# Attention in TensorE tiles of 64 rows by 32 columns, and blocks of 512 tokens, in front of two MLPs

## The chip, the core and the metric

The kernel runs on one core of one Trainium2 chip. The metric is the device time of one execution in microseconds. TensorE is called PE in the rows (PEld is its weight load), VectorE is DVE, ScalarE is ACT, GpSimd is POOL, and SyncE is SP, which issues the DMAs.

## The reference

For each of 4 batches and 8 heads, 768 queries of 64 elements are cut into 24 chunks of 32. A chunk attends to 8 memory keys and to its own neighbourhood: 16 keys to its left, its own 32, and 8 to its right, 64 keys in all (fewer at the ends). The result is a matrix of 3072 tokens by 512, which passes through two MLPs of hidden width 2048 in float32.

```
for c in range(nc):
    k_ctx = k[:, :, max(0, c*32 - 16) : min(S, c*32 + 32 + 8)]      # and v_ctx
    scores = scale * q_c @ concat(mem_k, k_ctx).T
    a = exp(scores - max(scores));  a = a / (sum(a) + 1e-9)
    out[:, :, c*32 : c*32 + 32] = a @ concat(mem_v, v_ctx)
x = out as [3072, 512]
x = silu(x @ w_in) @ w_out          # first MLP
x = relu(x @ w2_in)**2 @ w2_out     # second MLP
```

The weights are 64-bit floats; the kernel converts them on the chip.

## The kernel before, in words

**Precision.** The large products run as three matmuls in the format fp32r: each operand is split into a high part and a remainder (`high`, `low` pieces), and high x low, low x high, high x high are summed in PSUM. A matmul on plain float32 operands shows as two matmul records, each with a weight load of its own.

**First MLP and attention.** Tokens go in 8 blocks of 384 (`TB`). `mlp(j)` takes 16 steps a block; a step has 12 matmuls of 384 columns into the hidden tile (`hidden`, L738 to L740), Silu and the split (L746, L750, L753), and 12 matmuls back (`back`, L771 to L773). The attention of block j+1 is issued among the steps of block j. Its unit is one head of one block: 4 groups of 96 queries (3 chunks) against the 128 keys that any of the three sees. Blocks 0 and 1 take the plain path (`plain_pair`): float32 scores with the mask as three extra rows (L360), transposes on TensorE (L488), Exp (L494), the product with the values with a column of ones for the sums (L500), the division, and a transpose back (L527). The other six blocks take a path with fp32r scores (operands made at L328 to L342, matmuls L362 and L363), four Exp a unit (L389), the division (L396 to L398), eight 32x32-block transposes a unit on VectorE (L413), and one float32 product for two heads (L432), in which each head writes its own 64 output columns. Two heads are a pair; a block has four pairs.

**Block 0** runs while the weights of the first MLP arrive and are converted (`convert`, L545 to L610), so TensorE, ScalarE and VectorE are all loaded there. Before it stands a start-up stretch with nothing but the attention of block 0.

**Second MLP.** It runs in 6 blocks of 512 tokens: the first product by seven products of half size (`stage_in`, L904, 42 matmuls of 256 columns), the second by 12 matmuls of 512 columns a half (`stage_out`, L995 to L997). Its weights are converted during the last blocks of the first MLP (`convert_out`) and around the start of the second (`convert_forms`).

**The order of the work.** Every piece is an entry of a graph with a due time, its engine's cost, what it comes after, and the buffers that it takes from rings (`Graph.order`). A list scheduler places the ready piece with the earliest due time on a free engine; the placed order is the program order of each engine, so an engine waits in that order for what is late. A ring's next user comes after the users of the buffer that it takes over, and starts behind the ring's previous taker. PSUM has 8 banks: `acc` 4, `ph` 2, `sc` 1, `po` 1.

Of the kernel before, what the change touches and what calls it, by code (L numbers as in the profile page):

```python
# [13 lines left out]
F32 = mybir.dt.float32  # L14
# [12 lines left out]
GC = 3  # L27
GQ = GC * CHUNK
GK = NMEM + LEFT + GQ + RIGHT
NG = S // GQ  # L30
UG = 4
TB = UG * GQ
NHALF = NG // UG
NB = B * NHALF
NT = B * S
DM = H * D
# [4 lines left out]
NU = NB * H  # L41
QW, KW, VW = TB, UG * GK, UG * (D + 1)
MASKED = -float(2 ** 100)
# [8 lines left out]
F32_UNITS = 2 * H  # L52
# [8 lines left out]
PRODUCTS = (1, 6, 5, 7, 2, 3, 4)  # L61

# [120 lines left out]
def chunk_attention_two_mlps(ctx, tc, units, values, weights, consts, out):  # L183
# [12 lines left out]

    for i in range(FT):
        pool(f"w{i}")
    for tag, n in (
        ("raw", 3), ("v", 4), ("pr", 2), ("pts", 2), ("qk", 1), ("k20", 1), ("k21", 1),  # L200
        ("x", 2), ("g", 3), ("wraw", 2), ("wu", 4), ("wr", 3), ("y", 2), ("nm", 3), ("sm", 3),
    ):
        pool(tag, n)
    for tag, n in (("acc", 4), ("ph", 2), ("sc", 1), ("po", 1)):
        pool(tag, n, bass.MemoryType.PSUM)
# [17 lines left out]
    split = [G.buf(t) for t in ("qk", "k20", "k21")]  # L223
    qk = take(split[0], [P, 2 * QW + KW], F32R)
    q1, k1, q2 = qk[:, :QW], qk[:, QW:QW + KW], qk[:D + GC, QW + KW:]
    k2 = [take(b, [D + GC, KW], F32R) for b in split[1:]]


    FIRST, SLOW = 32.0, 95.0
    STEP1 = 4.97  # L230
# [11 lines left out]
    def unit_due(u):  # L242
        j, h = divmod(u, H)
        if j == 0:
            return FIRST - 2.2 * (H - 1 - h)
        at, to = step_due(j - 1, 0), step_due(j, 0)
        return at + (to - at) * (h + 1) / H - 2.0
# [3 lines left out]
    last_scores, pairs = [], []  # L251

    def const_loads():

        done = []
        for n, (dst, at) in enumerate([(q2, 0), (k2[0], QW), (k2[1], QW + KW)]):
            width, c = dst.shape[1], G.buf("v")

            def load(e, at=at, width=width, c=c):
                t = take(c, [P, KW], BF16)  # L260
                nc.sync.dma_start(out=t[D:D + GC, :width], in_=consts[:, at:at + width])

            def copy(e, dst=dst, width=width, c=c):
                nc.gpsimd.tensor_copy(dst[D:D + GC], c.tile[D:D + GC, :width])

            due = unit_due(F32_UNITS) - 40 + 3 * n
            a = G.add({"SP": 0.45}, due, load, new=[c], size=4000)
            done.append(G.add({"POOL": 1.3}, due + 2, copy, [a], uses=[c, *split]))
        return done

    turned = []

    def sees(c, k):

        first = NMEM + c * CHUNK
        last = NMEM + LEFT + (c + 1) * CHUNK + RIGHT
        return k * CHUNK < NMEM or k * CHUNK < last and (k + 1) * CHUNK > first

    def cleared(due):

        pts = G.buf("pts")

        def zero(e):
            t = take(pts, [P, TB], F32).rearrange("p (g q) -> p g q", g=UG)
            for k in range(GK // CHUNK):
                for c in range(GC):
                    if not sees(c, k):
                        ks, qs = slice(k * CHUNK, (k + 1) * CHUNK), slice(c * CHUNK, (c + 1) * CHUNK)
                        nc.gpsimd.memset(t[ks, :, qs], 0.0)

        return pts, G.add({"POOL": 1.2}, due, zero, new=[pts]), []

    def attend(u, masks, pair):
        j, h = divmod(u, H)
        half, plain, due = j % NHALF, u < F32_UNITS, unit_due(u)
        rows = D + GC if plain else P

        raw = G.buf(f"w{FT - H + h}" if j == 0 else "raw")
        v = raw if j == 0 else G.buf("v")

        def load(e):
            take(raw, [P, QW + KW + VW * (j == 0)], F32)
            r = D if plain else P
            nc.sync.dma_start(out=raw.tile[:r, :QW + KW], in_=units[u, :r])
            if plain:
                nc.sync.dma_start(out=raw.tile[D:rows, :QW + KW], in_=units[u, D:rows])

        def load_v(e):
            if j:
                take(v, [P, VW], F32)  # L310
            nc.sync.dma_start(out=v.tile[:, v_at:], in_=values[u])

        v_at = 0 if j else QW + KW
        got = G.add({"SP": 0.8 if plain else 0.4}, due - 28, load, new=[raw],
                    size=rows * (QW + KW) * 4)
        if j == 0:
            got_v = G.add({"SP": 0.4}, due - 22, load_v, uses=[raw], size=P * VW * 4)
            got_v.behind.append(got)
        else:
            got_v = G.add({"SP": 0.4}, due - 22, load_v, new=[v], size=P * VW * 4)  # L320
        ready = [got]
        if not plain:
            free = [got, *last_scores, *masks]

            def high(e):
                t = raw.tile
                q, k = t[:, 0:QW], t[:, QW:QW + KW]
                nc.gpsimd.tensor_scalar(q1, q, SCALE, 1.0, op0=ALU.mult, op1=ALU.mult)  # L328
                nc.gpsimd.tensor_scalar(k1, k, 1.0, 1.0, op0=ALU.mult, op1=ALU.mult)
                nc.gpsimd.tensor_scalar(  # L330
                    q2[0:D], q[0:D], SCALE, 1.0, op0=ALU.mult, op1=ALU.mult
                )

            def low_q(e):
                q = raw.tile[:, 0:QW]
                nc.vector.scalar_tensor_tensor(
                    q1[D:P], q[D:P], SCALE, f(q1[D:P]), op0=ALU.mult, op1=ALU.subtract
                )

            def low_k(e):  # L340
                k = raw.tile[:, QW:QW + KW]
                nc.vector.tensor_tensor(k2[half][0:D], k[0:D], f(k1[0:D]), op=ALU.subtract)  # L342

            a = G.add({"POOL": 1.9}, due - 17, high, free, uses=[raw, *split])
            b = G.add({"DVE": 0.75}, due - 15, low_q, [a], uses=[raw, *split], port=True)
            c = G.add({"DVE": 0.75}, due - 14.5, low_k, [a], uses=[raw, *split], port=True)
            ready = [b, c]

        tag = "acc" if j == 0 else "sc"
        sc, nm, pr = G.buf(tag), G.buf("nm"), G.buf("pr")  # L350
        sm = None if plain else G.buf("sm")

        def score(e):
            t = take(sc, [GQ, KW], F32)
            for g in range(UG):
                o = t[:, g * GK:(g + 1) * GK]
                qs, ks = slice(g * GQ, (g + 1) * GQ), slice(g * GK, (g + 1) * GK)
                if plain:
                    r = raw.tile[:rows, :QW + KW]
                    nc.tensor.matmul(o, r[:, qs], r[:, QW:][:, ks], start=True, stop=True)  # L360
                else:
                    nc.tensor.matmul(o, q2[:, qs], k2[half][:, ks], start=True, stop=False)  # L362
                    nc.tensor.matmul(o, q1[:, qs], k1[:, ks], start=False, stop=True)  # L363

        def top(e):
            t = take(nm, [GQ, UG], F32)
            nc.vector.tensor_reduce(
                t, sc.tile.rearrange("p (g k) -> p g k", g=UG), axis=AX.X, op=ALU.max, negate=True
            )

        s = G.add({"PE": 1.1 if plain else 0.7}, due - 11, score, ready, new=[sc],
                  uses=[raw] if plain else [raw, *split])
        last_scores[:] = [] if plain else [s]
        m = G.add({"DVE": 0.72}, due - 10, top, [s], new=[nm], uses=[sc])
        if plain:
            pair.append((u, sc, nm, pr, v, v_at, m, got_v))
            if h % 2:
                pairs.append((pair[:], due))
                pair.clear()

            while h % 2 and len(pairs) > (j == 0 and h < H - 1):
                plain_pair(*pairs.pop(0))
            return

        def exp(e):
            p = take(pr, [GQ, UG, GK], F32)
            s = take(sm, [GQ, UG], F32)
            for g in range(UG):
                nc.scalar.activation(  # L389
                    p[:, g, :], sc.tile[:, g * GK:(g + 1) * GK], AF.Exp,  # L390
                    bias=nm.tile[:, g:g + 1], accum_out=s[:, g:g + 1],
                )

        def norm(e):
            p, s = pr.tile, sm.tile
            nc.vector.tensor_scalar(s, s, EPS, 1.0, op0=ALU.add, op1=ALU.mult)  # L396
# [7 lines left out]
        if not turned:  # L404
            turned.extend(cleared(due - 40) for _ in range(2))
# [14 lines left out]
        if h % 2 == 0:  # L420
            return
# [714 lines left out]
```

## Time and profile before

| what | value |
|---|---|
| median of 3 runs (lowest to highest) | 1181.97 us (1181.8 to 1183.61) |
| profiled execution, its own time | 1181.42 us |
| its span, first to last instruction | 1179.4 us |
| busy: PE, DVE, ACT, POOL | 99%, 70%, 52%, 19% |
| DMA, share of 16 engines | 31.2% |

Busy time of TensorE counts a matmul from its issue to its modelled end, and matmuls overlap; so the pace is read from the distance between starts, not from the duration of one.

### The profile page before, as it was taken

How to read it: one execution, taken by the hardware profiler on the slowest of the kernel's cores; microseconds unless marked ns; L12 is line 12 of the kernel's file. 1: busy time of each engine (PE TensorE's matmuls, PEld its weight loads, DVE VectorE, ACT ScalarE, POOL GpSimd, SP SyncE). 2: the span in 40 equal slices, each digit the busy share in tenths (PEclk: the TensorE clock that was granted, in tenths of full speed). 3: DMA queues.
4: the chain of work that ended last, by engine and by line, in shares of the span. 5: the costliest groups of instructions: out<-in, count | busy, mean ns of one | idle time of the engine just before them, and what ended most of it. 6: DMA issues, size and time to landing. Idle time of an engine off the chain costs nothing.

```text
span 1179.4 us, 19661 instructions
## 1 busy us (share of the span) xinstructions
PE 1162.7 (99%) x7360; PEld 1098.5 (93%) x7360; DVE 831.2 (70%) x1748; ACT 616.7 (52%) x1296; POOL 221.6 (19%) x267
## 2 busy tenths in 40 slices
PE   8999999999999999999999999999999999999998
PEld 8998999999999999999999998899988898898987
DVE  5888867878777777778648587765756756756654
ACT  3899866766666666676646444323323223223321
POOL 0322211112111121121101232312202311311100
PEclk9999999999999999999999999999999999999999
DMA  9905322333323333353024323311312311321210
GB/s 244 373 25 178 109 70 93 119 120 104 128 72 119 107 100 106 103 164 99 1 72 134 126 69 93 116 55 54 118 44 54 126 48 48 120 54 54 79 48 36
DMA packets 57552, 117.45 MB, mean 100 GB/s; under 512 B 6201, under 2 KB 24642, under 8 KB 57458
## 3 DMA queue, kind: packets, MB, share of 16 engines
q1 hardware_dynamic: 57458, 116.20, 31.2%
q8 instruction: 58, 0.95, 0.3%
q14 instruction: 36, 0.29, 0.1%
HBM read 99.40 MB, written 16.78 MB: 99 GB/s over the span
## 4 chain that ended last, share of the span: by engine, by line
PE 94%; DVE 3%; ACT 1%; DMA 1%; issue 1%; POOL 0%; SPq 0%
PE pp L904 19%; PE ph L738 8%; PE acc L771 8%; PE ph L740 7%; PE ph L739 7%; PE acc L997 7%; PE acc L995 7%; PE acc L996 7%; PE acc L773 7%; PE acc L772 7%; PE po L432 2%; PE sc L362 1%; PE sc L363 1%; PE acc L360 1%; DVE g L954 1%; PE po L500 1%
## 5 line engine op out<-in xcount | busy, mean ns | idle before, releaser
L904 PEld LDWEIGHTS pp<-xs,forms 128*128 128x128 f32 x2016 | 246.9, 190 | 6.8 <-DVE sums L919 2.5
L904 PE MATMUL pp<-xs,forms 128*128 128x256 f32 x2016 | 249.1, 282 | 1.9 <-DVE sums L919 1.9
L738 PE MATMUL ph<-x,w 128*128 128x384 f32 x512 | 175.8, 343 | 1.9 <-DVE g L753 1.4
L771 PE MATMUL acc<-g,w 128*128 128x384 f32 x512 | 176.7, 345 | 0.0
L919 DVE TENSOR_TENSOR sums<-pp,sums 128x256 f32<-128x256 f32 x336 | 134.1, 421 | 60.3 <-PE pp L904 57.0
L950 ACT CAST g<-sums 128x512 fp32r<-128x512 f32 x96 | 59.6, 621 | 222.2 <-DVE sums L946 172.5
L739 PE MATMUL ph<-x,w 128*128 128x384 f32 x512 | 174.3, 340 | 0.0
L740 PE MATMUL ph<-x,w 128*128 128x384 f32 x512 | 174.2, 340 | 0.0
L773 PE MATMUL acc<-g,w 128*128 128x384 f32 x512 | 173.0, 338 | 0.0
L772 PE MATMUL acc<-g,w 128*128 128x384 f32 x512 | 172.8, 337 | 0.0
L997 PE MATMUL acc<-w,g 128*128 128x512 f32 x384 | 151.5, 395 | 0.0
L996 PE MATMUL acc<-w,g 128*128 128x512 f32 x384 | 151.4, 394 | 0.0
L995 PE MATMUL acc<-w,g 128*128 128x512 f32 x384 | 151.4, 394 | 0.0
L746 ACT ACTIVATE ph<-ph 128x384 f32<-128x384 f32 x128 | 60.6, 475 | 146.1 <-PE ph L740 143.5
L413 DVE STREAM_TRANSPOSE pts<-pr 32x128 f32<-32x128 f32 x384 | 115.6, 301 | 5.9
L975 POOL TENSOR_TENSOR w<-wf,w 128x512 fp32r<-128x512 f32 x44 | 58.1, 1325 | 301.7 <-ACT w L971 301.7
L753 DVE TENSOR_TENSOR g<-ph,g 128x384 fp32r<-128x384 f32 x128 | 70.7, 554 | 49.6 <-ACT g L750 47.6
L971 ACT CAST w<-wf 128x512 fp32r<-128x512 f32 x96 | 58.3, 622 | 86.6 <-PE acc L997 80.0
L738 PEld LDWEIGHTS ph<-x,w 128*128 128x128 f32 x512 | 97.1, 190 | 3.2 <-DVE g L753 1.9
L954 DVE TENSOR_TENSOR g<-sums,g 128x512 fp32r<-128x512 f32 x94 | 70.2, 750 | 40.0 <-ACT g L950 38.4
L771 PEld LDWEIGHTS acc<-g,w 128*128 128x128 f32 x512 | 96.3, 188 | 1.1
L740 PEld LDWEIGHTS ph<-x,w 128*128 128x128 f32 x512 | 97.1, 190 | 0.0
(113 smaller groups left out, 1937.4 us busy)
## 6 DMA issues: line engine op xcount, KB each, us to landing
wf<-w2s SPq DMA_DIRECT2D x96, 256.0 KB
raw<-units SPq DMA_DIRECT2D x48, 448.0 KB
wraw<-weights SPq DMA_DIRECT2D x40, 512.0 KB
w<-weights SPq DMA_DIRECT2D x24, 512.0 KB
v<-values SPq DMA_DIRECT2D x56, 130.0 KB
y<-y SPq DMA_DIRECT2D x32, 192.0 KB
xf<-y SPq DMA_DIRECT2D x24, 256.0 KB
w2s<-wu SPq DMA_DIRECT2D x16, 256.0 KB
```

The lines of the kernel that those rows point to most:

```text
L413: nc.vector.transpose(out=t[ks, :, qs], in_=pr.tile[qs, :, ks])
L738: nc.tensor.matmul(o, w[:, 1, ws], x[:, 0, kt], start=(kt == 0), stop=False)
L739: nc.tensor.matmul(o, w[:, 0, ws], x[:, 1, kt], start=False, stop=False)
L740: nc.tensor.matmul(o, w[:, 0, ws], x[:, 0, kt], start=False, stop=(kt == KT - 1))
L771: nc.tensor.matmul(o, w[:, 1, ws], t[:, 0], start=first, stop=False)
L772: nc.tensor.matmul(o, w[:, 0, ws], t[:, 1], start=False, stop=False)
L773: nc.tensor.matmul(o, w[:, 0, ws], t[:, 0], start=False, stop=last)
L904: nc.tensor.matmul(o, w[:, a, ws], t[:, c, kt], start=(kt == 0 and at == 0), stop=(kt == 1 and at == 2),)
L919: nc.vector.tensor_tensor(to.tile[:, t0:t1], bank[n].tile, other.tile, op=ALU.add)
L995: nc.tensor.matmul(o, t[:, 0, gs], w[:, 1], start=first, stop=False)
L996: nc.tensor.matmul(o, t[:, 1, gs], w[:, 0], start=False, stop=False)
L997: nc.tensor.matmul(o, t[:, 0, gs], w[:, 0], start=False, stop=last)
```

## The change

- The unit becomes a pair of heads of one block. Blocks have 512 tokens, so the first MLP has 6 blocks of 16 steps with 512 columns. All blocks take one path: float32 scores, transposes on TensorE, one Exp a pair, the product with the values, the division, a transpose back.
- Each chunk of 32 queries meets its own 64 keys, so no score has to be masked. One matmul has 64 rows (the elements of a head, or the keys) and 32 output columns (the queries); head a lies at rows 64a, chunk c at columns 32(c % 4): eight tiles of the array. The scores of a pair are 32 such matmuls with 64 moving columns, the product with the values 32 with 65.
- The host lays out queries, keys and values by chunks (`_units`): 8 halves of 644 KB a block in place of 8 units of 234.5 KB plus 8 of 130 KB in block 0, with keys repeated where chunks overlap. The masks and their loads are gone.
- PSUM: `po` goes, `sc` has two banks. Buffers and ring sizes in SBUF are moved about; in the second MLP the seventh sum of tokens and the fourth product's operand move into the tiles of the ring `x`, and the partial sums into `pr`, `pts` and `xq`.
- Twelve bf16 matmuls of 512 columns on ones stand at the very start (`warm`).
- `convert_out` begins 8 steps into block 1, and all eight `convert_forms` are created ahead of the last block in place of three after it and the rest between the steps of the second MLP. Their due times by the second MLP are as before. Piece costs and due times are set anew.

The core of the diff:

```diff
-GC = 3
+GC = 4
-GK = NMEM + LEFT + GQ + RIGHT
+KC = NMEM + LEFT + CHUNK + RIGHT
...
+    def warm(e):
+        t, o = take(dense, [P, WARM], F32), ones.tile
+        for _ in range(DENSE):
+            nc.tensor.matmul(t, o[:, :P], o, start=True, stop=True)
...
+        def score(e, n):
+            if n == 0:
+                for b in sc:
+                    take(b, [P, UG, KC], F32, "sc")
+            t = raw[n].tile
+            for c in range(UC):
+                g, rows = n * UG // 2 + c // GC, slice(c % GC * CHUNK, (c % GC + 1) * CHUNK)
+                for a in range(2):
+                    ds = slice(a * D, (a + 1) * D)
+                    nc.tensor.matmul(
+                        sc[a].tile[rows, g], t[ds, c * CHUNK:(c + 1) * CHUNK],
+                        t[ds, QW + c * KC:QW + (c + 1) * KC], start=True, stop=True,
+                    )
...
+        def turn(e, to, src):
+            t = take(to, [P, TB], F32, "turned")
             for g in range(UG):
...
+                nc.tensor.transpose(t[:, g * GQ:(g + 1) * GQ], src.tile[:, g], ident)
...
+                    for a in range(2):
+                        ks = slice(a * KC, (a + 1) * KC)
+                        nc.tensor.matmul(
+                            po[a].tile[rows, g], pts.tile[ks, at:at + CHUNK],
+                            raw[n].tile[ks, vs], start=True, stop=True,
+                        )
...
-            shared, at = rank in (4, 5, 6), max(0, rank - 4)
-            new = not triple or not shared
+            shared, at = rank > 2, max(0, rank - 3)
+            new = not four or not shared
...
+        if j == NB - 1:
+            for k in range(PAIRS):
+                convert_forms(k)
         y = mlp(j)
     row.append(y)
-    for i in range(FT):
-        convert_out(i)
-    for k in range(3):
-        convert_forms(k)
     second()
```

## Rows read from the trace of the kernel before

**Rows 1.** The page: busy time by engine, and the chain's shares by engine.

```profile
PE 1162.7 (99%) x7360; PEld 1098.5 (93%) x7360; DVE 831.2 (70%) x1748; ACT 616.7 (52%) x1296; POOL 221.6 (19%) x267
...
PE 94%; DVE 3%; ACT 1%; DMA 1%; issue 1%; POOL 0%; SPq 0%
```

**Rows 2.** Busy by stretch: length, PE, PEld, DVE, ACT, POOL, clock, DMA, GB/s.

```profile
0.00:39.20 39.20, 33.75 (x184) 33.03 (x185) 23.50 (x52) 15.03 (x28) 3.48 (x9) 1.00 0.94 271
39.20:130.00 90.80, 88.62 (x562) 86.48 (x562) 75.15 (x137) 84.05 (x149) 27.67 (x33) 0.98 0.47 161
130.00:664.30 534.30, 531.03 (x3450) 521.47 (x3449) 393.62 (x914) 351.24 (x814) 85.94 (x145) 1.00 0.31 100
664.30:1179.40 515.10, 509.35 (x3170) 457.53 (x3168) 338.93 (x647) 166.42 (x308) 104.53 (x81) 1.00 0.24 75
```

**Rows 3.** What PE waited for: us in total, times, longest.

```profile
PE po L432 <- DVE pts L413: 1.8, 1, 1.8
```

**Rows 4.** The chain that ended last, in order of time: start, us, what.

```profile
17.31 3.41 PE acc L360 x16
...
162.23 0.81 PE po L432 x16
...
472.88 0.81 PE po L432 x16
...
664.61 10.27 PE pp L904 x84
```

**Rows 5.** PE in order of time, MLP matmuls: start, us, instruction.

```profile
39.21 0.67 PE L738 MATMUL ph<-x,w 128*128 128x384 f32 x1
...
146.58 0.34 PE L738 MATMUL ph<-x,w 128*128 128x384 f32 x1
...
152.74 0.34 PE L740 MATMUL ph<-x,w 128*128 128x384 f32 x1
...
706.46 0.39 PE L995 MATMUL acc<-w,g 128*128 128x512 f32 x1
...
711.80 0.40 PE L997 MATMUL acc<-w,g 128*128 128x512 f32 x1
```

**Rows 6.** PE in order of time, attention pieces and the MLP records beside them.

```profile
56.62 1.04 PE L360 MATMUL sc<-raw 67*96 67x128 f32 x8
...
57.67 0.34 PE L739 MATMUL ph<-x,w 128*128 128x384 f32 x1
...
68.06 0.49 PE L488 MATMUL po<-ident,pr 96*128 96x96 f32 x4
...
68.59 0.34 PE L772 MATMUL acc<-g,w 128*128 128x384 f32 x1
...
72.64 0.82 PE L500 MATMUL po<-v,pts 128*96 128x65 f32 x8
...
73.53 0.34 PE L772 MATMUL acc<-g,w 128*128 128x384 f32 x1
...
161.89 0.34 PE L740 MATMUL ph<-x,w 128*128 128x384 f32 x1
162.16 0.88 PE L432 MATMUL po<-pts,v 128*64 128x96 f32 x16
162.97 0.30 PE L362 MATMUL sc<-k,qk 67*96 67x128 f32 x1
```

**Rows 7.** Two stretches of 10 ns, matmuls of L432 alone (x counts those in flight).

```profile
162.16:162.17 0.01, 0.01 (x2) 1.00 0.00 0
...
162.30:162.31 0.01, 0.01 (x4) 1.00 0.00 0
```

**Rows 8.** Groups by line and shape: weight loads of 96 and of 64 columns.

```profile
L363 PEld LDWEIGHTS sc<-qk 128*96 128x96 f32 x192 | 31.3, 163 | 0.5
...
L432 PEld LDWEIGHTS po<-pts,v 128*64 128x64 f32 x384 | 17.0, 136 | 7.3 <-issue 4.8 <-DVE pts L413 2.1
```

More of the change, by code (lines that the diff above doesn't have):

```diff
@@ L61 @@
 PRODUCTS = (1, 6, 5, 7, 2, 3, 4)
+WARM, DENSE = 512, 12
 class Buf:
@@ L182, in chunk_attention_two_mlps @@
 @with_exitstack
-def chunk_attention_two_mlps(ctx, tc, units, values, weights, consts, out):
+def chunk_attention_two_mlps(ctx, tc, units, weights, out):
     nc = tc.nc
@@ L222, in chunk_attention_two_mlps, with fill @@
     make_identity(nc, ident)
[L223 to L230, printed above, removed]
+    ones, dense = G.buf("x"), G.buf("ph")
+    def fill(e):
+        nc.vector.memset(take(ones, [P, WARM], BF16, "ones"), 1.0)
+    def warm(e):
+        t, o = take(dense, [P, WARM], F32), ones.tile
+        for _ in range(DENSE):
+            nc.tensor.matmul(t, o[:, :P], o, start=True, stop=True)
+    a = G.add({"DVE": 0.3}, -100.0, fill, new=[ones])
+    G.add({"PE": 4.0}, -100.0, warm, [a], new=[dense], uses=[ones])
+    FIRST, SLOW = 34.0, 96.0
+    STEP1 = 6.15
     BLOCK1 = FT * STEP1
@@ L240, in step_due, with unit_due @@
         return FIRST + SLOW + (j - 1) * BLOCK1 + i * STEP1
-    def unit_due(u):
-        j, h = divmod(u, H)
+    def unit_due(j, p):
         if j == 0:
-            return FIRST - 2.2 * (H - 1 - h)
+            return FIRST - 3.0 * (HP - 1 - p)
         at, to = step_due(j - 1, 0), step_due(j, 0)
-        return at + (to - at) * (h + 1) / H - 2.0
+        return at + (to - at) * (p + 1) / HP - 8.0
     x_buf, x_done = {}, {}
[L251 to L331, printed above, removed]
-                )
[L334 to L354, printed above, removed]
-            for g in range(UG):
[L356 to L383, printed above, removed]
-        def exp(e):
[L386 to L396, printed above, removed]
@@ L409, in blocks @@
-        def blocks(e, some):
-            t = pts.tile.rearrange("p (g q) -> p g q", g=UG)
-            for k, c in some:
-                ks, qs = slice(k * CHUNK, (k + 1) * CHUNK), slice(c * CHUNK, (c + 1) * CHUNK)
-                nc.vector.transpose(out=t[ks, :, qs], in_=pr.tile[qs, :, ks])
-        mid = len(seen) // 2
-        a = G.add({"DVE": 1.2}, due - 5.5, lambda e: blocks(e, seen[:mid]), [n, clear, *readers],
-                  uses=[pr, pts])
-        b = G.add({"DVE": 1.2}, due - 4, lambda e: blocks(e, seen[mid:]), [a], uses=[pr, pts])
@@ L419, in attend @@
-        pair.append((v, pts, [b, got_v], readers))
-        if h % 2 == 0:
-            return
-        two = pair[:]
-        pair.clear()
-        po = G.buf("po")
-        def weigh(e):
-            t = take(po, [P, TB], F32)
-            for g in range(UG):
-                qs, ks = slice(g * GQ, (g + 1) * GQ), slice(g * (D + 1), (g + 1) * (D + 1) - 1)
-                for n, (v, pts, _, _) in enumerate(two):
-                    nc.tensor.matmul(
-                        t[n * D:(n + 1) * D, qs], v.tile[:, ks], pts.tile[:, qs],
-                        start=True, stop=True,
-                    )
@@ new lines, in weigh_values @@
+        done = []
+        for a in range(2):
+            done.append(G.add({"DVE": 0.43}, due - 10, lambda e, a=a: less(e, a),
+                              [tops[a], *done], new=[pr] if a == 0 else (),
+                              uses=[sc[a], nm] + ([pr] if a else [])))
+        d = G.add({"PE": 0.55}, due - 9, lambda e: turn(e, pt, pr), done, new=[pt], uses=[pr])
+        d = G.add({"ACT": 0.64}, due - 8, exp, [d], new=[pts], uses=[pt], table="exp")
+        d = G.add({"PE": 1.0}, due - 6, weigh, [d, *got_v], new=po, uses=[pts, *raw])
@@ L447, in split_x @@
+        done = []
+        for a in range(2):
+            sm = G.buf("sm")
+            done.append(G.add({"DVE": 0.85}, due - 5, lambda e, a=a, sm=sm: norm(e, a, sm),
+                              [d, *done], new=[sm] + [xq] * (a == 0),
+                              uses=[po[a]] + [xq] * (a == 1)))
+        d = G.add({"PE": 0.55}, due - 3, lambda e: turn(e, back, xq), done, new=[back], uses=[xq])
+        split_x(j, p, back, d, due)
+    def split_x(j, p, po, done, due):
         new = []
@@ L889, in stage_in @@
         bank = {n: G.buf(next(in_bank)) for n in PRODUCTS}
-        s1, u2, u4, u3 = [G.buf("v") for _ in range(4)]
-        h = [G.buf(next(h_place)) for _ in range(2)]
+        left, right = (0, HALF2), (HALF2, T2)
+        one, two = G.buf("pr"), G.buf("pts")
+        s1, u2, u4, u3 = (one, left), (one, right), (two, left), (two, right)
+        h = [G.buf("xq") for _ in range(2)]
         made = {}
@@ L1012, in second @@
             if n is None:
-                if b == 0 and k + 3 < PAIRS:
-                    convert_forms(k + 3)
                 if k == 0:
@@ L1024, in second @@
             if (k, n) == (last, 1):
-                evict(accs[b], y, due, DM,
-                      lambda m, b=b: out[b * T2 + m * P:b * T2 + (m + 1) * P, :])
-    pair, masks = [], []
-    for u in range(H):
-        attend(u, masks, pair)
+                evict(accs[b], y, due,
+                      lambda m, b=b: out[b * T2 + m * P:b * T2 + (m + 1) * P, :], b == NB2 - 1)
+    waiting = []
+    for p in range(HP):
+        waiting.append(attend(0, p))
+        if p:
+            weigh_values(*waiting.pop(0))
+    weigh_values(*waiting.pop(0))
     for i in range(FT + 2):
```

324 lines of the change are left out of this document (143 added, 181 removed).

## The prediction

> **What bounds the kernel now.** I read the page first, then the table by stretches, then what TensorE waited for, then the chain, and last the matmul starts. The page says that TensorE is busy in 99% of the span and makes up 94% of the chain [rows 1]: the time is the sum of what TensorE's instructions take, so each part is priced by the distance between matmul starts. The stretches [rows 2] are the start-up (39.2 us, DMA at 0.94 share), block 0 with the conversion of the weights (ScalarE 84 of 91 us), the other seven blocks of the first MLP, and the second MLP (515 us). VectorE has slack beyond block 0: 394 of 534 us.
>
> **The first MLP stage, split.** It runs from the first hidden matmul at 39.21 [rows 5] to the first matmul of the second MLP at 664.61 [rows 4]: 625.4 us.
> - MLP matmuls: from 146.58 to 152.74 lie 35 intervals, 0.1760 us each [rows 5]. There are 8 x 16 x 24 = 3072: 540.7 us.
> - Attention of six blocks: the same product of a block recurs every (472.88 - 162.23)/4 = 77.66 us [rows 4]. Less 384 x 0.1760 = 67.6 leaves 10.1 us a block, 2.52 a pair, 60.5 for 24 pairs.
> - The four float32 pairs beside block 0. A piece costs the time from its first record to the second MLP record behind it, less one interval [rows 6]: scores of a head 57.67 - 56.62 - 0.176 = 0.87, transposes 0.35, product 0.71, and once a pair a transpose back (taken as 0.35). So 2 x 1.94 + 0.35 = 4.24 a pair, 17.0 in all.
> - The rest, 625.4 - 540.7 - 60.5 - 17.0 = 7.2 us, is waits and time at the lower of the clock's two levels (granted clock 0.98 over block 0 [rows 2]).
>
> **The change, part by part.**
>
> *MLP matmuls of 512 columns.* The second MLP has such matmuls: from 706.46 to 711.80 lie 23 intervals, 0.2322 us each [rows 5]. There will be 6 x 16 x 24 = 2304: 535.0 us, 5.7 less.
>
> *Attention on TensorE, per pair.* Float32 streams at 0.874/8/128 = 0.85 ns a column and record (L360 [rows 6]). Two records a matmul and 32 matmuls make 64 records for the scores, and as many for the product with the values. What decides is whether the eight tiles work side by side. L432 is the only row with parts of the array: two heads, 64 columns each. Its 16 records of 96 columns would need 16 x 96 x 0.85 = 1.31 us one after the other, but the next piece starts 0.81 us after the first record [rows 6]. In the 10 ns from 162.16 two of its matmuls are in flight, and 0.14 us later four, in two pairs [rows 7]. So two column parts run side by side: eight rounds of two. I carry this over to eight tiles. The scores are then eight rounds of 64 columns: 8 x 64 x 0.85 = 0.44 us. Changing over costs what L432 shows beyond its rounds: it begins 162.16 - 161.89 - 0.176 = 0.09 late and lasts 0.81 for 0.66 of rounds, 0.25 in all. So the scores take 0.69, the product the same. A transpose piece of 128 columns in place of 96 takes 0.354 x 128/96 = 0.47, and there are two. Sum: 2 x 0.69 + 0.94 = 2.32 us a pair. Only blocks 1 to 5 have attention beside MLP steps, so 20 pairs: 46.4 us, in place of 77.5.
>
> Bounds for a pair: from below 1.8, if the changeovers hide. From above, if each record has to wait its turn at the weight load: a load of 96 columns lasts 163 ns and one of 64 lasts 136 [rows 8], 0.84 ns a column, so 27 ns for 32; 128 x 0.027 + 1.44 (changeovers and transposes) = 4.9 us. If records keep L432's mean distance (0.66/16 = 41 ns), 6.7. I take 2.3, because the one row with tiles shows them side by side.
>
> [...] The trace has no row of tiles this small; the two matmuls that begin within one 10 ns stretch [rows 7] speak against a fixed distance between starts, but not against a mean one.
>
> *Waits and clock.* The one long wait of L432 for VectorE's transposes (1.8 us [rows 3]) goes with them; the other 5.4 us of the rest I keep. What VectorE and ScalarE do for a pair gets less (no operand splits, no block transposes, one Exp in place of up to eight), and they stand beside TensorE beyond block 0 [rows 2]. In block 0 ScalarE gets 16 larger Silu and copy pieces and fewer changes of its table; cover is that the block now takes TensorE about 100 us. If that cover fails, the block is some 10 us longer (a rival). PSUM's ring `sc` now carries scores, transposes and products of a pair in turn, six takings of two banks; a pair has a quarter of a block, 25 us, so what would be late is a piece placed too early in TensorE's order; such waits are in the 5.4.
>
> *Start-up.* Before, TensorE is at it nearly all of 39.2 us at half pace: 16 records of L360 take 3.41 us (213 ns each [rows 4]), eight later ones 0.874 (109 ns). The records' granted clock says 1.00 there, so I go by the pace. After: data for four pairs is 8 x 644 KB = 5.28 MB, at the stretch's mean of 271 GB/s [rows 2] 19.5 us, plus 3 that I allow for issue and landing. Then the last pair's chain: about ten pieces on three engines, each of the order of those in [rows 6], with their hand-overs: I allow 12 us. First hidden matmul at 35, between 31 (data alone) and 39 (no gain). The weights come behind 2.2 MB more, 8 us later; they have this cover too, since the first conversion needs only one of 32 loads. The twelve `warm` matmuls run before any data has landed: nothing, unless they hold the clock up (in the lower end).
>
> *Second MLP.* Its matmuls are unchanged: 515 us kept. The fourth product's operand must now wait for the previous block's last product in place of its fourth; cover are three `stage_out` pieces of 12 x 0.2322 = 2.8 us, and without it up to 1 us a block, 5 in all. The eight `convert_forms` now stand ahead of the second MLP's weight loads in their ring; cover is the last block, in which no attention is left to do. Without it the first `stage_out` waits, up to 5 us. The earlier `convert_out`, the host's layout and the DMAs of a block (16, as before) hide in stretches with DMA at a third. Both ways I take 0.
>
> **The sum.** First stage: 535.0 + 46.4 + 5.4 = 586.8. The second MLP starts at 35 + 586.8 = 621.8, that is 42.8 earlier. On the profiled execution's own 1181.4 (span 1179.4) that gives 1138.6; the median shown lies 0.5 above that execution: **1139 us**.
>
> **The rivals.**
> - *The records queue.* Eight tiles don't run side by side: weight loads or issue set a distance between records. This one ends slower. Its place is the 20 pairs beside MLP steps. For it: two tiles are all that this trace shows, and they alternate in program order, as the new ones do. Against: pairs start within 10 ns [rows 7]. At 27 ns a record, 4.9 a pair: 1139 + 20 x 2.58 = 1191 us. It decides where a pair costs 2.32 + 42.8/20 = 4.46, i.e. from (4.46 - 1.44)/128 = 24 ns a record. Chance 0.15; 0.02 of it falls about zero. [...]
> - *Block 0 and the start hold on to what they take.* The data lands late (first matmul at 39, 4 us) and ScalarE or VectorE sets the pace of block 0 (10 us, with four thirds of the tokens): 1153 us. For it: both are near full there [rows 2]. Against: attention leaves them work. Chance 0.11.
> - *The clock falls beside the small tiles.* Each pair throws TensorE to its lower level, for as long as cost block 0 (1 - 0.98) x 90.8 = 1.8 us [rows 2]: 1.8 x 20 = 36, 1175 us. For it: the pace at start-up, where only attention ran. Against: 1.00 from 130 on, with four pairs a block [rows 2]. Chance 0.04.
> - My forecast: 0.70. Its own range goes from 1126 (a pair at 1.8, start at 31, 2 to 3 of the waits gone) to 1152 (a pair at 2.9 with the scores split into two pieces, start at 37).
>
> **How the numbers follow.** The range is 1125 to 1175: the forecast's own and the second rival, and the third at its end; the queue of records, 0.15, stays out. This kernel's runs can tell a change of 0.2% (2.4 us) from none. Faster: 0.70 + 0.11 + 0.04 - 0.01 for mishaps at the edge = 0.84. Slower: 0.13. Same: 0.03.
>
> **What would show it.** Right: hidden matmuls 0.232 us apart; 64 score records within 0.7 us, many in flight at once; a block of the first MLP at 384 x 0.2322 + 4 x 2.3 = 98.4 us; the first hidden matmul near 35; the second MLP still 515 us. Wrong: score records 25 ns or more apart (then blocks of 108 us); waits of TensorE for ScalarE or VectorE in block 0, or at the second MLP's start for converted weights; MLP records twice as far apart behind attention pieces.

## The result and the profile after

The changed kernel takes 1163.1 us in the median of 4 runs (1162.39 to 1164.41), beside 1181.88 for the kernel before on the same chip (1180.18 to 1183.61). The ratio is 0.9842, with a 95% interval of 0.9825 to 0.9859. The change makes the kernel faster, and the time lies in the range given; but the gain is 18.8 us where 42.9 were forecast. The profiled execution took 1163.26 us, its span is 1161.4.

The page after: busy time of each engine, and the chain by engine, which answer to [rows 1].

```profile
PE 1133.4 (98%) x8748; PEld 943.0 (81%) x8748; DVE 614.6 (53%) x1207; ACT 459.2 (40%) x780; POOL 120.1 (10%) x98
...
PE 93%; issue 3%; DVE 3%; ACT 0%; POOL 0%; DVEq 0%; POOLq 0%
```

TensorE still sets the time. VectorE falls from 70% to 53%, ScalarE from 52% to 40%: the change frees both, and that is worth little, because they make up 3% and 0% of the chain. The same stretches as in [rows 2], cut at the first hidden matmul, at block 1's and at the second MLP (length, PE, PEld, DVE, ACT, POOL, clock, DMA share, GB/s):

```profile
0.00:35.90 35.90, 20.50 (x556) 13.56 (x557) 15.90 (x48) 8.12 (x13) 1.96 (x7) 0.77 0.97 371
35.90:146.50 110.60, 104.28 (x930) 81.43 (x929) 81.80 (x140) 83.07 (x141) 18.05 (x14) 0.98 0.41 148
146.50:644.00 497.50, 497.50 (x4098) 390.72 (x4097) 191.71 (x400) 212.69 (x339) 6.92 (x7) 1.00 0.30 97
644.00:1161.40 517.40, 511.16 (x3169) 457.31 (x3167) 325.16 (x620) 155.27 (x287) 93.14 (x70) 1.00 0.23 71
```

Three things are to be seen. In the start-up TensorE is now idle for 15 of 36 us. Block 0 has 6.3 us without TensorE, more than the 2.2 of the stretch before. From 146.5 to 644 there is no gap at all; what is too long there is in the instructions themselves. The chain in order of time gives the price of a block: the product of one place in the order recurs.

```profile
160.73 0.79 PE po L357 x53
...
541.97 0.79 PE po L357 x53
...
644.20 9.98 PE pp L780 x84
```

Between the first two lie 15 pairs, each with the four MLP steps beside it: 381.24/15 = 25.42 us. The pace of the MLP matmuls is read where no attention stands beside them, in the last block:

```profile
553.74 0.39 PE L618 MATMUL ph<-x,w 128*128 128x512 f32 x1
...
643.80 0.40 PE L653 MATMUL acc<-g,w 128*128 128x512 f32 x1
```

These are 386 intervals in 90.06 us, 0.2333 us each. Four steps are 96 x 0.2333 = 22.40, so a pair costs **3.02 us**, where 2.52 was the price before [rows 4] for a pair of heads in a block of three quarters of the tokens, and 2.32 the forecast. Sorted by the forecast's terms, on the profiled execution:

| term | forecast | measured | more |
|---|---|---|---|
| first hidden matmul at | 35 | 35.9 | 0.9 |
| 2304 MLP matmuls | 535.0 | 537.5 | 2.5 |
| 20 pairs | 46.4 | 60.4 | 14.0 |
| rest of the first stage (644.0 less the three above) | 5.4 | 10.2 | 4.8 |
| second MLP to the end | 516.8 | 519.3 | 2.5 |
| time | 1138.6 | 1163.3 | 24.7 |

**Where a pair's time goes.** TensorE in order of time after: an MLP matmul, one of a pair's two score pieces (32 records), two MLP matmuls; further down the product (64 records) between the same neighbours.

```profile
198.37 0.40 PE L653 MATMUL acc<-g,w 128*128 128x512 f32 x1
198.70 0.45 PE L298 MATMUL sc<-raw 64*32 64x64 f32 x32
...
199.42 0.40 PE L619 MATMUL ph<-x,w 128*128 128x512 f32 x1
...
211.17 0.39 PE L653 MATMUL acc<-g,w 128*128 128x512 f32 x1
211.49 0.86 PE L357 MATMUL po<-raw,pts 64*32 64x65 f32 x64
212.28 0.50 PE L618 MATMUL ph<-x,w 128*128 128x512 f32 x1
212.62 0.39 PE L619 MATMUL ph<-x,w 128*128 128x512 f32 x1
```

From the MLP record ahead of the scores to the second one behind are 1.05 us, of which two intervals of 0.2333 would be there anyway: a score piece costs 0.58. The product costs 1.45 - 0.467 = 0.98 in the same way. Over the steady stretch (160 to 540 us) the medians are 0.58 for each of two score pieces, 0.44 for each of two transposes, 0.98 for the product: all of the 3.02. What stands around the records of a small-tile piece is the same each time: the first one starts 0.09 late (211.49 - 211.17 - 0.2333), the next MLP matmul comes 0.15 behind the last record's start, and the second MLP matmul 0.10 late. That is **0.34 a changeover, and there are three in a pair**. It counts from the last record's start; without that record's own 0.055 us (64 columns at the forecast's 0.85 ns; the last rounds of eight of a score piece start 0.055 apart too) it is 0.285.

The tiles themselves do work side by side. Matmuls in flight (x) in stretches of 10 ns, for the score line alone:

```profile
198.70:198.71 0.01, 0.01 (x2) 1.00 0.00 0
198.74:198.75 0.01, 0.01 (x8) 1.00 0.00 0
198.79:198.80 0.01, 0.01 (x11) 1.00 0.00 0
```

Eight records are in flight 40 ns after the first, one every 6.7 ns, and the piece's 32 records all start within 0.24 us. (x counts records begun and, by the trace's model, not ended; with eight tiles in the piece, eleven in flight share some of them.) The product's 64 do not go on like that. Its records begun up to three moments (length of the stretch, busy, x):

```profile
211.40:211.73 0.33, 0.24 (x31) 1.00 0.00 0
211.40:211.97 0.57, 0.48 (x48) 1.00 0.00 0
211.40:212.30 0.90, 0.81 (x64) 1.00 0.00 0
```

31 records begin in the first 0.24 us, only 17 in the next 0.24; the last starts 0.64 after the first, so that the run takes 0.70 with that record's own 0.055. Eight rounds of 64 columns would have been 0.44.

**The hole after block 0.** TensorE in order of time at the end of block 0, with what it waited for in brackets:

```profile
141.90 0.63 PE L341 MATMUL turned<-ident,pr 128*128 128x128 f32 x4 [1.68 <-DVE pr L333]
143.21 0.86 PE L357 MATMUL po<-raw,pts 64*32 64x65 f32 x64 [0.69 <-ACT pts L344]
145.81 1.09 PE L341 MATMUL turned<-ident,xq 128*128 128x128 f32 x4 [1.74 <-DVE xq L368]
146.55 0.77 PE L618 MATMUL ph<-x,w 128*128 128x512 f32 x1
147.12 0.63 PE L619 MATMUL ph<-x,w 128*128 128x512 f32 x1
147.55 0.63 PE L620 MATMUL ph<-x,w 128*128 128x512 f32 x1
```

From its second score piece on (139.77) block 1's last pair is done in one go, transposes, product and transposes back, with no MLP step between them to cover VectorE and ScalarE. Behind it MLP matmuls are 0.43 us apart in place of 0.23 (147.12 to 147.55): the granted clock from 146.55 to 149.05 is 0.50, the lower of the two levels that the traces of both kernels show (1.00 and 0.50), after TensorE had waited three times for 0.7 to 1.7 us. The loads say why the pair stands there: SyncE issues the load of its first half at 105, that of its second only at 127.14, behind the product of the pair before (126.6) that gives the buffer up: two pairs' four halves share three buffers, and the planner takes a load for slow.

### The profile page after: what moved, and what is told of

The parts are those of the page before. It is cut to its first block, busy times and chain, and to the rows that moved or that the text cites. A ratio compares the mean times of both kernels' runs of the same rounds, so it can differ in the third digit from the quotient of the medians.

```text
span 1161.4 us, 20995 instructions
## 1 busy us (share of the span) xinstructions
PE 1133.4 (98%) x8748; PEld 943.0 (81%) x8748; DVE 614.6 (53%) x1207; ACT 459.2 (40%) x780; POOL 120.1 (10%) x98
## 4 chain that ended last, share of the span: by engine, by line
PE 93%; issue 3%; DVE 3%; ACT 0%; POOL 0%; DVEq 0%; POOLq 0%
PE pp L780 20%; PE ph L618 8%; PE acc L651 8%; PE acc L653 8%; PE acc L652 8%; PE ph L620 7%; PE acc L871 7%; PE acc L872 7%; PE acc L870 7%; PE ph L619 7%; PE turned L341 2%; PE po L357 2%; PE sc L298 1%; DVE sums L821 1%; PE ph L233 0%
## 5 line engine op out<-in xcount | busy, mean ns | idle before, releaser
L626 ACT ACTIVATE ph<-ph 128x512 f32<-128x512 f32 x96 | 55.9, 582 | 262.0 <-PE ph L620 261.9
L618 PE MATMUL ph<-x,w 128*128 128x512 f32 x384 | 157.6, 410 | 1.0 <-POOL w L487 1.0
L651 PE MATMUL acc<-g,w 128*128 128x512 f32 x384 | 156.4, 407 | 0.0
L633 DVE TENSOR_TENSOR g<-ph,g 128x512 fp32r<-128x512 f32 x96 | 65.9, 687 | 167.7 <-ACT g L630 167.3
L620 PE MATMUL ph<-x,w 128*128 128x512 f32 x384 | 153.2, 399 | 0.0
L619 PE MATMUL ph<-x,w 128*128 128x512 f32 x384 | 152.3, 397 | 0.0
L653 PE MATMUL acc<-g,w 128*128 128x512 f32 x384 | 152.1, 396 | 0.0
L652 PE MATMUL acc<-g,w 128*128 128x512 f32 x384 | 151.2, 394 | 0.0
L618 PEld LDWEIGHTS ph<-x,w 128*128 128x128 f32 x384 | 73.0, 190 | 19.7 <-POOL w L487 1.4
L620 PEld LDWEIGHTS ph<-x,w 128*128 128x128 f32 x384 | 72.8, 190 | 17.7
L653 PEld LDWEIGHTS acc<-g,w 128*128 128x128 f32 x384 | 72.1, 188 | 17.5
L872 PEld LDWEIGHTS acc<-w,g 128*128 128x128 f32 x384 | 72.1, 188 | 17.3
```

The lines of the kernel that those rows point to most:

```text
L618: nc.tensor.matmul(o, w[:, 1, ws], x[:, 0, kt], start=(kt == 0), stop=False)
L619: nc.tensor.matmul(o, w[:, 0, ws], x[:, 1, kt], start=False, stop=False)
L620: nc.tensor.matmul(o, w[:, 0, ws], x[:, 0, kt], start=False, stop=(kt == KT - 1))
L651: nc.tensor.matmul(o, w[:, 1, ws], t[:, 0], start=first, stop=False)
L652: nc.tensor.matmul(o, w[:, 0, ws], t[:, 1], start=False, stop=False)
L653: nc.tensor.matmul(o, w[:, 0, ws], t[:, 0], start=False, stop=last)
```

## The experiments

**1. What made the hole.** `PIPE` is the rate, in MB per us, at which the planner lets loads land. It says 2.9 us for a half of 644 KB; the start-up shows 371 GB/s. With 0.38 the plan places block 1's pairs earlier. One edit, in the changed kernel:

```
-    PIPE, LANDING = 0.23, 1.8
+    PIPE, LANDING = 0.38, 1.8
```

> The planner's rate for loads goes from 0.23 to 0.38 MB/us; no instruction changes, only their order. Theory (the plan makes the loads of block 1's queries late, so that its last pair stands alone between blocks 0 and 1): block 1's pairs lie between steps 0.5 and 14.5 of block 0, TensorE's waits of 1.7, 0.7 and 1.7 us at 141 to 146 us go, with the half pace behind them; 1156 to 1158 us. Rival (the data really comes that late): new waits of TensorE for the units' loads inside block 0, and 1163 us.

Measured: 1154.59 us (1153.69 to 1155.24), ratio to the kernel before 0.9771 [0.9756, 0.9785], 8.5 us less than the change and a little more gain than expected. TensorE at the end of block 0 of this kernel:

```profile
127.08 0.86 PE L357 MATMUL po<-raw,pts 64*32 64x65 f32 x64
...
130.77 0.60 PE L341 MATMUL turned<-ident,xq 128*128 128x128 f32 x4
...
136.81 0.40 PE L618 MATMUL ph<-x,w 128*128 128x512 f32 x1
```

The last pair's pieces now lie 3 to 4 us apart among MLP steps, none of them waits, and block 1 begins at 136.81 in place of 146.55, with one step's 12 matmuls back of block 0 (2.8 us) still to come. A later block costs what it did before this edit (101.66 us). The hole was the plan's, not the hardware's. The rest of the first stage falls to 635.86 - 35.80 - 537.5 - 60.4 = 2.2 us, below the 5.4 forecast.

**2. The same edit in the kernel before.** A rival said that this is simply a better planner constant and owes nothing to the change.

```
-    PIPE, LANDING = 0.23, 1.8
+    PIPE, LANDING = 0.38, 1.8
```

> The kernel before with the planner's rate for loads at 0.38 in place of 0.23 MB/us. Theory (the lone last pair between blocks 0 and 1 came with the change: a pair now holds two of three buffers of 644 KB, and the plan thinks that each load takes 2.9 us): the kernel before has no such hole to lose, its waits in block 0 are 3 us in all; 1178 to 1183 us. Rival (the plan's rate cost both kernels the same): 1174 us or less.

Measured: 1189.87 us, ratio 1.0067 [1.0052, 1.0082]: slower. The first hidden matmul moves from 39.2 to 42.5, and TensorE waits longer than before (us in total, times, longest):

```profile
PE pp L904 <- DVE sums L919: 4.3, 5, 1.1
...
PE ph L738 <- POOL w L610: 2.8, 3, 2.5
```

The rival falls, and the 1178 to 1183 expected here was missed too. A truer rate is no gain by itself: the order that it makes is another one, better in the changed kernel, whose old order had a hole, and worse here. Why it is worse was not followed further than these waits.

**3. One changeover less.** On top of experiment 1 the two score pieces of a pair become one.

```
-        for n in range(2):
-            scored.append(G.add({"PE": 0.5}, due - 12, lambda e, n=n: score(e, n),
-                                [got[n], *scored], new=sc if n == 0 else (),
-                                uses=[raw[n]] + (sc if n else [])))
+        def both_scores(e):
+            score(e, 0)
+            score(e, 1)
+
+        scored.append(G.add({"PE": 1.0}, due - 12, both_scores, got, new=sc, uses=raw))
```

> As the run before, and the two score pieces of a pair become one of 64 records. Theory (a piece of small tiles pays 0.34 us of changing over, and beyond the first 32 or so records TensorE can only issue one each 17 ns): a pair gets 0.18 us cheaper, 25.24 us for a pair and four steps, 3.5 us less than the run before. Rival (only changing over costs): 0.34 us a pair, 25.08 us, 6.9 us less. Rival (changing over hides): no change.

Measured: 1150.78 us (1150.72 to 1151.88), ratio 0.9741 [0.9727, 0.9756], 3.8 less than experiment 1. TensorE around a score piece of this kernel:

```profile
239.14 0.40 PE L654 MATMUL acc<-g,w 128*128 128x512 f32 x1
239.47 0.86 PE L298 MATMUL sc<-raw 64*32 64x64 f32 x64
...
240.59 0.39 PE L620 MATMUL ph<-x,w 128*128 128x512 f32 x1
```

1.45 - 0.467 = 0.98, the product's price: 64 records cost that whether they are scores or product, in place of 2 x 0.58. A pair and its four steps recur every 25.24 us in place of 25.42, as the theory had it. So the merge saves a changeover of 0.34 and gives half of it back, since the longer run starts its second half of records more slowly, as the product does above (31, then 17 records in 0.24 us). The theory's 17 ns a record is not what the trace shows: behind its first 32 the product's records start some (0.64 - 0.24)/32 = 12.5 ns apart in the mean.

**4. One changeover more.** On top of experiment 1 the product is cut into two pieces of 32 records, half an MLP step apart.

```
...
-        d = G.add({"PE": 1.0}, due - 6, weigh, [d, *got_v], new=po, uses=[pts, *raw])
+        w = [G.add({"PE": 0.5}, due - 6, lambda e: weigh(e, 0), [d, *got_v], new=po,
+                   uses=[pts, raw[0]])]
+        later = 2.0 if j else 0.0
+        d = G.add({"PE": 0.5}, due - 6 + later, lambda e: weigh(e, 1), [d, *got_v, *w],
+                  uses=[pts, raw[1], *po])
...
```

> As the run with the faster loads in the plan (1154.6 us), and the product of a pair in two pieces of 32 records, half a step apart, in place of one of 64. Theory (0.34 us of changing over a piece, and 17 ns a record beyond the first 32 or so of a piece): each half costs 0.58 us as a score piece does, a pair 0.18 us more, 25.60 us for a pair and four steps, 1158 us. Rival (the product's records are slow for their own sake, 10 ns each, and only changing over is added): 0.34 us a pair, 25.76 us, 1161.5 us.

Measured: 1157.67 us (1156.96 to 1158.07), ratio 0.9793 [0.9776, 0.9809], 3.1 more than experiment 1. In order of time, the halves in this kernel:

```profile
254.99 0.46 PE L358 MATMUL po<-raw,pts 64*32 64x65 f32 x32
...
258.38 0.46 PE L358 MATMUL po<-raw,pts 64*32 64x65 f32 x32
```

Each costs 0.59, like a score piece, and a pair and its four steps recur every 25.60 us. Experiments 3 and 4 move the count of changeovers by one a pair in either direction and the time follows by -3.8 and +3.1: 0.15 to 0.19 a pair and no more, as the prices of 32 and of 64 records say (2 x 0.58 - 0.98 = 0.18). Both edits change the number of pieces and the length of a run together; how a price divides between the two is read from the trace alone.

**5. Two tiles at a time.** The chunks are taken in an order in which two in a row lie in the same columns of the array, so that each group of eight records meets only two of the eight tiles. If TensorE kept strictly to the order, most of the working side by side would be lost.

```
-            for c in range(UC):
+            for c in (0, 4, 1, 5, 2, 6, 3, 7):
```

(in the scores and in the product)

> The changed kernel with the chunks in the order 0, 4, 1, 5, 2, 6, 3, 7, so that four matmuls in a row use the same two tiles of the array. Theory (tiles run side by side, but records start in program order): two tiles at a time, 56 ns a round; 32 score records take 0.9 us for 0.24 and the 64 of the product 1.8 for 0.64, 2.5 us a pair, 20 pairs: 1212 us. Rival (TensorE starts later matmuls past a busy tile): below 1185. Rival (tiles are not what counts, a record costs its issue): 1163.

Measured: 1169.18 us in one run, 6 above the change. The score line's matmuls in flight in 10 ns, of this kernel:

```profile
200.88:200.89 0.01, 0.01 (x2) 1.00 0.00 0
200.92:200.93 0.01, 0.01 (x4) 1.00 0.00 0
200.97:200.98 0.01, 0.01 (x10) 1.00 0.00 0
```

The score piece takes 0.62 for 0.58, the product 1.15 for 0.98: 0.24 a pair, 4.9 us in 20 pairs. 40 ns in, 4 records are in flight and not 8, but 90 ns in there are 10. Strictly in order, 32 records would be four groups of four rounds on two tiles, an estimated 16 x 64 x 0.85 ns = 0.87 us, or 13 rounds and 0.71 us if the last round of a group runs beside the first of the next. The whole piece costs less, 0.62 with changing over included. The two estimates rest on 0.85 ns a column on a small tile too, which is carried over from larger ones (L360 [rows 6]); that a later record goes past an earlier one at a busy tile was not shown record by record. The in-order theory, with its 1212 us, falls; the order of the tiles is worth 0.24 us a pair here.

**6. Weight loads later.** Is the start-up held up by 32 weight loads that share the DMA with the units? All but the first were made to wait for the scores of block 0's last pair.

```
+        if (j, p) == (0, HOLD):
+            hold.append(scored[-1])
...
+        if (i, c) != (0, 0):
+            got.after += hold
```

> All weight loads but the first wait for the scores of block 0's last pair. Theory (at the start TensorE's instructions come late because their fetches share the DMA engines with the weights): the waits that no semaphore ends (2.3, 0.7 and 3.3 us at 12, 20 and 24 us) shrink to under 2 us in all, the first hidden matmul comes at 31 to 33 us for 35.9, and the whole gains 2 to 4 us unless the weights then come too late. Rival (the fetch takes its time however free the DMA engines are): the same waits, 1163 us or more.

Measured: 1165.09 us (1164.73 to 1165.58), ratio 0.986 [0.9843, 0.9876]. The first hidden matmul stays at 35.92. The DMA was no freer for it, since the units' own loads fill it (some 400 GB/s from 8 us on, as before the edit). So this tells nothing of what the start would do on a free DMA, and the stops described below changed only from 6.3 to 5.6 us. That they are late fetches, as the theory had it, was not shown. Open.

**7. No warm-up.** The twelve matmuls on ones, and the tiles they use, are taken out; the change's output does not depend on them.

```
...
-    a = G.add({"DVE": 0.3}, -100.0, fill, new=[ones])
-    G.add({"PE": 4.0}, -100.0, warm, [a], new=[dense], uses=[ones])
```

> The changed kernel without the twelve bf16 matmuls at its start. Theory (the start is set by the data and by each pair's chain through three engines, TensorE at half pace or not): the first scores run at half pace (13 ns a record in a round for 7), the first hidden matmul comes at 36 to 37.5 us for 35.9; 1163 to 1165 us. Rival (the full pace of the first 12 us is worth as much as it lasts): first hidden matmul at 39 or later, 1166 us or more.

Measured: 1160.18 us (1159.9 to 1161.85), ratio 0.9817 [0.98, 0.9833], 2.9 less than the change. Neither expectation held. The first hidden matmul is at 32.39 in place of 35.91. The start-up with the warm-up, in the changed kernel:

```profile
1.45 4.85 PE L233 MATMUL ph<-ones 128*128 128x512 bf16 x12 [1.45 <-DVE ones L228]
6.23 0.86 PE L298 MATMUL sc<-raw 64*32 64x64 f32 x64
...
14.47 0.63 PE L298 MATMUL sc<-raw 64*32 64x64 f32 x19 [2.29 <-issue]
...
23.03 0.81 PE L357 MATMUL po<-raw,pts 64*32 64x65 f32 x59 [0.37 <-ACT pts L344]
27.11 0.43 PE L357 MATMUL po<-raw,pts 64*32 64x65 f32 x5 [3.27 <-issue]
```

The same view of the kernel without the warm-up:

```profile
3.90 0.68 PE L284 MATMUL sc<-raw 64*32 64x64 f32 x32 [3.90 <-DMA raw<-units]
...
22.82 1.19 PE L343 MATMUL po<-raw,pts 64*32 64x65 f32 x64
```

Three things are seen. The warm-up matmuls do stand in the way of landed data: the first scores start at 6.23 with them and at 3.90 without. But by the third product only 0.2 us of that is left (23.03 and 22.82). And they do not hold the pace: from 35.90 to 39.80 us the granted clock of the changed kernel is 0.50, and its MLP matmuls are some 0.43 apart there. Then there is "issue": TensorE stands still from 12.18, 20.15 and 23.84 us with nothing to wait for that the profile shows, for 2.3, 0.7 and 3.3 us. The third stop falls into the middle of a product, 5 matmuls short of its end. Without the warm-up that product runs through, and this is nearly all of the 3.5 us by which the first hidden matmul comes earlier. The whole kernel keeps 2.9 of it.

**8. A short warm-up.** Is it the warm-up's time or its number of instructions? Twelve matmuls of 128 columns keep the number.

```
-WARM, DENSE = 512, 12
+WARM, DENSE = 128, 12
```

> The changed kernel with twelve matmuls of 128 columns on ones in place of 512: as many TensorE instructions, a quarter of the time. Theory (TensorE stands still at each 256th of its instructions at the start, and the 24 of the warm-up move one such stop into the third pair's product): stops at the same instructions, 3 us in the third product, first hidden matmul still at 35.5 to 36, 1163 us. Rival (what costs is that TensorE is taken up to 6.2 us, when the data is there at 3.9): first hidden matmul at 32 to 33.5, 1160 us.

Measured: 1163.9 us (1162.77 to 1165.44), ratio 0.9848 [0.9829, 0.9867]: no gain over the change, though the first hidden matmul is 0.94 us earlier (34.97). That lead is lost before block 1, which begins at 147.51 in place of 146.55: the granted clock of this kernel is 0.50 from 60.20 to 63.50 us, where the change has 1.00. In order of time, the third product of this kernel:

```profile
23.18 1.15 PE L357 MATMUL po<-raw,pts 64*32 64x65 f32 x59
26.15 0.43 PE L357 MATMUL po<-raw,pts 64*32 64x65 f32 x5 [1.82 <-issue]
```

It stops at the same instruction, 59 of 64, although its scores start at 3.87 us. So where the stops fall goes here by the count of instructions, not by time (the theory's 256 is what the changed kernel's trace counts between two stops, at the end of this text), and removing the 24 instructions of the warm-up (matmuls and weight loads) is what moves the third stop out of the product.

**9. All that gained, together**: experiments 1, 3 and 7.

> The planner's rate at 0.38, one score piece a pair, and no matmuls on ones at the start. Theory (the three gains lie in different stretches: the end of block 0, the pairs, the start): first hidden matmul at 32 to 33 us, a pair and four steps 25.24 us, 1147 to 1149 us. Rival (the start's gain hangs on where the fetches of instructions fall, and this order puts one in the way again): first hidden matmul at 35 and 1150 to 1152 us.

Measured: 1148.89 us (1148.61 to 1148.98), ratio 0.9724 [0.9709, 0.9739]. That is in the range of the theory, though the first hidden matmul is at 33.36, later than the 32 to 33 expected. It beats both kernels: 32.6 us less than the kernel before (1181.45 beside it) and 14.2 less than the change. Of experiment 7's 2.9 us only 1.9 are left on top of experiment 3; this version has its own stop of 2.9 us in a score piece.

## Why the prediction was right in direction and wrong in size

- **TensorE is the bound, and fewer MLP instructions pay: right.** 2304 matmuls at 0.2333 us, forecast at 0.2322: the slower pace takes 2.5 us of the 5.7 that were to be gained here. The first hidden matmul came at 35.9, forecast at 35, but that is in part luck: TensorE waited 0.3 us in all for the units' data, the first term of the 35, and stood 6.3 us in stops that the forecast did not have.
- **The price of a pair, 2.32: the term that failed most.** It is 3.02, 14.0 us in 20 pairs, and three steps of the sum made it. First the count: the diff issues the scores in two pieces, and the sum priced one run, so "0.25 in all" for the changeover is counted twice where it comes three times: 0.25. (The upper end of the forecast's own range had the split, as "a pair at 2.9".) Second its size, 0.285 for 0.25 in the forecast's terms, in which the last record's own time belongs to the rounds: 0.11 in three. The 0.25 came from the one L432 row whose next record is another attention piece, L362 [rows 6], in place of an MLP matmul. Where L432 stands between MLP records in the kernel before, it is 0.09 late, the next matmul comes 0.18 behind the last record's start, and the second is 0.10 late: 0.37, or 0.29 without that record's 0.08. So the price stood in the same trace:

```profile
280.36 0.34 PE L773 MATMUL acc<-g,w 128*128 128x384 f32 x1
280.62 0.88 PE L432 MATMUL po<-pts,v 128*64 128x96 f32 x16
281.44 0.44 PE L771 MATMUL acc<-g,w 128*128 128x384 f32 x1
281.71 0.34 PE L772 MATMUL acc<-g,w 128*128 128x384 f32 x1
```

- **"I carry this over to eight tiles": right that they run side by side, too fast as a rate.** This is the third step, and the largest. 32 records take 0.29 us for four rounds of 0.22 in all; the 64 of the product take 0.70 for the 0.44 of "8 x 64 x 0.85": the sum took the rate of a short run for a long one, and L432's 16 records [rows 6] could not show that. It makes 0.41 a pair. The transposes, 0.44 for 0.47, take 0.07 back: 0.25, 0.11 and 0.41 less 0.07 are the 0.70 that a pair is off. Experiments 3 and 4 bear out the prices of 32 and of 64 records.
- **"the other 5.4 us of the rest I keep": wrong, 10.2.** The text named what would do it, "a piece placed too early in TensorE's order", and priced it within the 5.4. Here a pair was placed too late, by a planner that takes a load for slow, and no cover was left at the block's end; waits for VectorE and ScalarE in block 0, and MLP records at half pace behind them, were among the forecast's own signs of being wrong. Experiment 1 brings the rest to 2.2, 8.0 us less.
- **The twelve `warm` matmuls "run before any data has landed: nothing": wrong.** Data landed at 3.90 us (experiment 7), and leaving them out gains 2.9. What they cost is less their time than their number: a quarter of the time with all the instructions gains nothing (experiment 8).
- **"515 us kept" for the second MLP: 2.5 short.** The MLP matmuls of the second product are 0.2338 us apart in the mean, in place of 0.2322 [rows 5], over 1152 of them some 2 us; behind the last of them the span goes on for 5.0 us in place of 3.8, and the waits for sums are 0.7 shorter. The feared waits (the fourth product's operand, `convert_forms`) are not in the table of waits. The slower pace is the changed kernel's own: its trace shows 0.2333 in the first MLP (as do experiments 1, 3 and 4) and 0.2338 in the second, the kernel before 0.2322 in the second. With the first MLP's share it costs some 4.4 us of the 24.7. Why is open; no run was made for it.
- **The rival of the queue of records: rejected.** 27 ns a record, or the 24 from which it decided, are not there: 32 records start in 0.24 us (7.4 ns each), 64 in 0.64 (10 ns). The 25 ns among the signs of being wrong, and the blocks of 108 us worked out from it, no run shows either: a block beside the MLP takes 4 x 25.42 = 101.7 us. All these records lie on different tiles; no row shows one tile by itself.
- **Block 0 and the start: the first matmul came earlier than the rival had it, but block 0 did take 12 us more than the 98.4 forecast** (110.6), near the rival's size. The cause is not the one named: ScalarE has 28 us of slack in that stretch, and with another order (experiment 1) the same work takes 103.8 (101.0 to block 1's first matmul and the 2.8 still to come).
- **The clock beside the small tiles: rejected.** The granted clock is 1.00 in the mean from 146.5 to 644, with four pairs a block in it. Where it did fall to 0.50, behind the hole, TensorE had been waiting (1.7, 0.7 and 1.7 us).

## What to carry to other kernels

Price a piece of small work between large matmuls by the whole detour, from the large record before to the second one behind, in a row where it stands between just those neighbours and has the length it will have; then multiply by the number of pieces that the code issues, not by the number of things computed. When work moves in a planned order, read that order around block ends: a constant that takes loads for slow cost here nearly half as much as the change gained, and the same constant set right harmed the kernel whose order had no hole. Work put at the start to fill idle time is not free: here its 24 instructions moved a stop of 3.3 us into the middle of a product. Take it out once and look.

## What the runs showed of the hardware

- Records on different small tiles start 6.7 ns apart (8 in flight after 40 ns), and some 32 in a row keep near to that (7.4 ns each); a run of 64 slows to about half that rate in its middle (31, then 17 records in 0.24 us). Why is open.
- With each group of eight records on two of the eight tiles a score piece took 0.62 us in place of 0.58, and the product 1.15 in place of 0.98 (experiment 5). Strict order on two tiles would need 0.71 or more for the score piece, by the estimate there.
- Going from 128x128 matmuls to small tiles and back costs some 0.29 us a piece beyond the records' own time, for tiles of 64x32 (0.285, changed kernel) and of 128x64 (0.29, L432 in the kernel before) alike; a piece of four 128x128 transposes (0.44 us) costs hardly more than its records, which start 0.109 apart.
- In the first 30 us TensorE stood still at fixed places of its program, 0.2 to 3.3 us each. Counts of the changed kernel between stops (length, PE with its matmuls, PEld with its loads, DVE, ACT, POOL, clock, DMA share, GB/s):

```profile
0.00:14.46 14.46, 8.56 (x221) 4.35 (x222) 4.74 (x15) 1.88 (x2) 0.70 (x6) 0.93 0.89 321
14.46:20.80 6.34, 4.99 (x127) 3.66 (x126) 3.54 (x11) 1.19 (x2) 0.00 (x0) 0.61 1.04 402
```

  221 matmuls lie ahead of the first stop and 127, with 126 loads and 3 semaphore instructions, between it and the second, 256 instructions in all; to the third there are 127 again, with 128 loads and 1 semaphore instruction, 256 once more. With the short warm-up and without any the counts to the first two stops are the same, at other times. The third place is 475 matmuls in; without the warm-up the third product ends with the 468th, and the place falls behind a wait of 2.07 us for VectorE that is there anyway. Between 10 and 30 us the queue of kind instruction moves three packets of 16 KB. What the stops wait for was not shown: experiment 6, meant to test it on a freer DMA, did not make the DMA free (some 400 GB/s from 8 us on).
